# Output projection by seven Strassen products, 512-token blocks with paired PSUM banks, and an interleaved load of batch 1 in a fused attention and bilinear FFN kernel

## The chip, the cores and the metric

The kernel runs on one core of a Trainium2 chip. The metric is the device time of one execution in microseconds (us), given as the median over the runs of one kernel. A run more than 1.5% above the fastest of its kernel is called slow and is left out of every ratio. Two kernels are called different where the interval of the ratio, or the two intervals, leave no room for equality. The engines are PE (TensorE, matmul), PEld (its weight loads, which overlap with PE), DVE (VectorE), ACT (ScalarE), POOL (GpSimd) and SP (SyncE). PE writes its results into PSUM, here eight banks (the tiles `bk`, 128 partitions by 512 float32 values); copying them out to SBUF, where all other tiles lie, is called evacuation. The granted clock is the share of its full clock that the profile shows as granted to PE.

## The reference

The input has 8 batches, 8 heads, 576 positions and a head dimension of 64; the FFN has 4608 tokens, d_model 512 and d_ff 1536.

```python
kv  = einsum('bhsd,bhse->bhde', k, v)
o   = einsum('bhsd,bhde->bhse', q, kv)
x   = o / sqrt(mean(o * o, -1) + 1e-6) * g_norm      # per token and head
x   = x.transpose(0, 2, 1, 3).reshape(4608, 512)
out = ((x @ w_a) * (x @ w_b)) @ w_out                # float32
```

## The kernel before

Attention writes normalised tokens to a ring `xp` (fp16, features on the partitions). The first 512 tokens pass through the FFN in the standard way. The other tokens go in six blocks of 2n tokens, n = 256, 320 or 384, where the two products `x @ w_a` and `x @ w_b` are each computed with seven half-size products instead of eight, in the arrangement by Strassen and Winograd. It needs four sums of weights, made once (`sums`), and four sums of token blocks (`T`), made per block on DVE. The output projection is standard: 12 products of 512 columns per 128 tokens.

Instructions are not issued in the order of the code. Each is a node of a plan with an estimated duration, a priority and its dependencies; a list scheduler (`Plan.order`) fixes the order on each engine at build time. The helper lines under which the profile lists instructions are marked here.

```python
# attention of a late batch: k is reordered on DVE, then K-V, then per head pair and half
r = plan.add("DVE", 1.2, w0, reorder, [(load["n"], 7.0)], [kr], [kb])      # kr_t <- k_t (L556, L559)
n = plan.add("PE", 1.6, w0, kv_mm, [r, (load["n"], 8.0), plan.at(w0 - 3)], [s, kd], [kr, vb])   # L570
#   x_mm (PE L329) -> square (ACT L339) -> mean over head (PE L343) -> rsqrt (ACT L347)
#   -> xp = x * g * rs (DVE L352)
...
first_us = 18.0 if dep is None else 7.0        # batch 2's load has no dep
ld["n"] = plan.add("POOL", first_us, prio, issue, ...)
...
for f0, f1 in zip(WB[:-1], WB[1:]):            # order of the loads: all of w_a, w_b, ...
    nc.gpsimd.dma_start(out=wa_t[:, :, f0:f1], in_=wa_v[:, :, f0:f1])
    nc.gpsimd.dma_start(out=wb_t[:, :, f0:f1], in_=wb_v[:, :, f0:f1])
for i in range(2):                             # ... then batch 1, then w_out
    early_load(early[1], 1, slice(i * HP, (i + 1) * HP))
...
# token sums of a Strassen block, on DVE (L712): T0 = b12-b11, T1 = b22-T0, T2 = b22-b12, T3 = b21-T1
# seven products into banks X, Y, Z of n columns, first for w_a, then for w_b (L734):
p1 = pe(0.0, X, w_lo, fs, lambda: b11, True, xdeps(lo, t0, t0 + n), [X])
e1 = ev(0.0, u1, X, p1)                        # ACT: u1 <- X (L758)
p2 = pe(0.1, Y, w_hi, fs, lambda: b21, True, xdeps(hi, t0, t0 + n), [Y])
c11 = comb(0.1, 0, 0, Y, u1, [p2, e1], ...)    # DVE: abt or b_sb <- Y + u1 (L764)
p6 = pe(0.2, X, sm[1], fs, lambda: tt(1), False, ...)   # goes on accumulating in X
...                                            # p5 in Z, p7 and p4 in X, p3 in Z
nc.vector.tensor_mul(t, t, bb.tile[...])       # abt <- abt * b_sb (L796)
...
# output projection, all blocks (L829), then a copy to SBUF on DVE or ACT (L862) and a store
nc.tensor.matmul(ps.tile[:], lhsT=ab.tile[:, f, g * 128:(g + 1) * 128], rhs=wo_t[:, f, :], ...)
```

Of the kernel before, what the change touches and what calls it, by code (L numbers as in the profile page):

```python
# [40 lines left out]
class Buf:  # L41
# [6 lines left out]
    def take(self, t=0.0):  # L48
        r = self.ring
        i = r.pool.pick()[1]  # L50

        self.tile = r.pool.tiles[i]
        r.pool.holder[i] = self
        r.held = [b for b in r.held if b.freed() > t] + [self]
        return self


class Node:
    def __init__(self, eng, dur, prio, emit, deps=(), takes=(), frees=()):
        self.eng, self.dur, self.prio, self.emit = eng, dur, prio, emit  # L60
        self.deps = [d if isinstance(d, tuple) else (d, None) for d in deps if d is not None]
        self.takes = takes
        self.start = self.end = None
        for b in frees:
            b.last.append(self)


class Plan:
# [29 lines left out]
    def order(self):  # L98
        free, todo, done = {}, sorted(self.nodes, key=lambda n: n.prio), []
        waits = {n: [d for d, _ in n.deps if d.end is None] for n in todo}  # L100
        while todo:
            best = {}
            for n in todo:
                if waits[n]:
                    waits[n] = [d for d in waits[n] if d.end is None]
                    if waits[n]:
                        continue
                f = free.get(n.eng, self.t0)
                if n.eng in best and best[n.eng][0][0] <= f:
                    continue  # L110
                t = max(self.ready(n), f)
                if t == INF:
                    continue
                key = (f if t < f + 0.06 else t, n.prio)
                if n.eng not in best or key < best[n.eng][0]:
                    best[n.eng] = (key, t, n)
            assert best, "no node can go"
            _, t, n = min(best.values(), key=lambda x: x[1])
# [10 lines left out]
def kernel(  # L129
# [27 lines left out]
    WB = [0, 128] + list(range(256, d_ff + 1, 256))  # L157
# [3 lines left out]
    BLOCKS = [(512, 320), (1152, 256), (1664, 320), (2304, 384), (3072, 384), (3840, 384)]  # L161
    NMAX = 384
    NJ = FC // 2

# [5 lines left out]
    def sb(name, shape, dt):  # L170
# [7 lines left out]
    sums = {w: [sb(f"s{w}{i}", [128, 2, HM], FP16) for i in range(4)] for w in "ab"}  # L178
    xp = [sb(f"xp{i}", [128, 2, R], FP16) for i in range(2)]
    k_ts = [sb(f"k_t{i}", [128, H * EC * D], BF16) for i in range(2)]  # L180
    v_ts = [sb(f"v_t{i}", [128, H * EC * D], BF16) for i in range(2)]
# [3 lines left out]
    T_ts = [sb(f"T{i}", [128, 4, 2, NMAX], FP16) for i in range(2)]  # L185
    b_ts = [sb(f"b_sb{i}", [128, 2, 2 * NMAX], FP16) for i in range(2)]
    u_ts = [sb(f"u{i}", [128, NMAX], FP32) for i in range(8)]
    sq_ts = [sb(f"sq{i}", [128, HF], BF16) for i in range(4)]
    rs_ts = [sb(f"rs{i}", [128, HF], FP32) for i in range(4)]
    o_ts = [sb(f"o_sb{i}", [128, d_model], FP32) for i in range(4)]  # L190

    arenas = [
        [ab_ts[1][:].rearrange("p a b -> p (a b)"), 0],
        [T_ts[0][:].rearrange("p a b c -> p (a b c)"), 0],
        [T_ts[1][:].rearrange("p a b c -> p (a b c)"), 0],
        [b_ts[1][:].rearrange("p a b -> p (a b)"), 0],
    ]

    def carve(n, dt=BF16):
        w = n * (2 if dt == FP32 else 1)  # L200
        for a in arenas:
            if a[1] + w <= a[0].shape[1]:
                ap = a[0][:, a[1] : a[1] + w].bitcast(dt)
                a[1] += w
                return ap
        raise ValueError(n)
# [4 lines left out]
    def early_load(t, b, hs):  # L211
        for n, src in (("q", q), ("k", k), ("v", v)):
# [6 lines left out]
        {  # L219
            "q": early_view(carve(H * EC * D)),  # L220
            "k": early_view(k_ts[b]),
            "v": early_view(v_ts[b]),
        }
        for b in range(2)
# [4 lines left out]
    for n, src, eng in (("q", q, nc.scalar), ("k", k, nc.sync), ("v", v, nc.sync)):  # L229
        raw[n] = carve(2 * EC * D, FP32)[0:EP].rearrange("p (h c d) -> p h c d", h=2, d=D)  # L230
# [6 lines left out]
    qs = [[carve(S) for _ in range(NP)] for _ in range(2)]  # L237


    zt = const.tile([128, 512], BF16)  # L240
# [24 lines left out]
    for f0, f1 in zip(WB[:-1], WB[1:]):  # L265
# [3 lines left out]

    for i in range(2):  # L270
        early_load(early[1], 1, slice(i * HP, (i + 1) * HP))
# [128 lines left out]

    N0 = BLOCKS[0][0]

# [58 lines left out]
    def fast_us(n):  # L461
        return (n / 2 + 100) / 960
# [6 lines left out]
    RU, RB, RT, RAB = Ring(u_ts), Ring(b_ts), Ring(T_ts), Ring(ab_ts)  # L469
    RSQ, RRS, ROS = Ring(sq_ts), Ring(rs_ts), Ring(o_ts)  # L470
    RK, RV, RKR, RQT, RKD = Ring(k_ts), Ring(v_ts), Ring([kr_t]), Ring(qT_ts), Ring(kvd[::-1])
# [12 lines left out]
    readers = {}  # L484

# [33 lines left out]
    def early_batch(b, win):  # L519
# [5 lines left out]
        for p in range(NP):  # L525
            pr = w0 + (w1 - w0) * (p - 0.7) / NP
            sq, sk = Buf(RY), Buf(RY)
            here = [plan.at(37.0 if p < NP // 2 else 40.5)]
# [14 lines left out]
    def late_batch(b, load, win):  # L543
# [17 lines left out]
        r = plan.add("DVE", 1.2, w0, reorder, [(load["n"], 7.0)], [kr], [kb])  # L561
        s = Buf(RS)

        def kv_mm():
# [14 lines left out]
            "PE", 1.6, w0, kv_mm, [r, (load["n"], 8.0), plan.at(w0 - 3)], [s, kd], [kr, vb]  # L579
# [14 lines left out]
    def load_node(b, prio, dep):  # L594
# [23 lines left out]
        def transpose():  # L618
# [5 lines left out]
        first_us = 18.0 if dep is None else 7.0  # L624
# [4 lines left out]
            "SP", 2.5, prio, transpose, [(ld["n"], 5.0)], [ld["q"]]  # L629
        )  # L630
        return ld
# [4 lines left out]
    def std_block(win):  # L636
# [4 lines left out]
        rd = readers.setdefault(0, [])  # L641
        for fc in range(2, FC):
            pr = w0 + (w1 - w0) * (fc - 2) / (FC - 2)
            pa, pb = Buf(RX), Buf(RY)

            def mm(ps, w, fc):
# [4 lines left out]
                "PE", mm_us(KC, N0), pr, lambda fc=fc, ps=pa: mm(ps, wa_t, fc), [tk], [pa]  # L651
# [5 lines left out]
                "PE", mm_us(KC, N0), pr + 0.01, lambda fc=fc, ps=pb: mm(ps, wb_t, fc), [tk], [pb]  # L657
# [5 lines left out]
        return ab, muls  # L663

    def weight_sums(prio):
        out = {}
        for w, t in (("a", wa_t), ("b", wb_t)):
            a11, a21 = t[:, 0:2, 0:HM], t[:, 0:2, HM:]
            a12, a22 = t[:, 2:4, 0:HM], t[:, 2:4, HM:]
            s1, s2, s3, s4 = sums[w]  # L670
            for i, (o, x, y, op) in enumerate(
                (
                    (s1, a21, a22, nc.vector.tensor_add),
                    (s2, s1[:], a11, nc.vector.tensor_sub),
                    (s3, a11, a21, nc.vector.tensor_sub),
                    (s4, a12, s2[:], nc.vector.tensor_sub),
                )
            ):
                out[w, i] = plan.add(
                    "DVE", fast_us(2 * HM), prio + 2 * i,  # L680
                    lambda o=o, x=x, y=y, op=op: op(o[:], x, y),  # L681
                    [out[w, i - 1]] if i else [plan.at(32.0)],
                )
        return out

    def wino_block(bi, win, wsum):
        t0, n = BLOCKS[bi - 1]
        w0, w1 = win
        c0 = t0 % R
        b11, b21 = (xp[i][:, :, c0 : c0 + n] for i in range(2))  # L690
        b12, b22 = (xp[i][:, :, c0 + n : c0 + 2 * n] for i in range(2))
        lo, hi = (0, 1), (2, 3)
        rd = readers.setdefault(bi, [])
        tb, ab = Buf(RT), Buf(RAB)
        tk = plan.add("V", 0.0, w0 - 9, lambda: None, (), [ab])

        def tt(i):
            return tb.tile[:, i, :, 0:n]

        t_n = []  # L700
        for i, (x, y, op, pairs, cols) in enumerate(
            (
                (lambda: b12, lambda: b11, nc.vector.tensor_sub, lo, (t0, t0 + 2 * n)),
                (lambda: b22, lambda: tt(0), nc.vector.tensor_sub, hi, (t0 + n, t0 + 2 * n)),
                (lambda: b22, lambda: b12, nc.vector.tensor_sub, lo + hi, (t0 + n, t0 + 2 * n)),
                (lambda: b21, lambda: tt(1), nc.vector.tensor_sub, hi, (t0, t0 + n)),
            )
        ):
            t_n.append(
                plan.add(  # L710
                    "DVE", fast_us(2 * n), w0 - 6 + i,
                    lambda i=i, x=x, y=y, op=op: op(tt(i), x(), y()),  # L712
                    xdeps(pairs, *cols) + ([t_n[0]] if i == 1 else [t_n[1]] if i == 3 else []),
                    [tb] if i == 0 else (),
                )
            )
        rd += t_n
        muls = {}
        for j in range(NJ):
# [5 lines left out]
            outs = []  # L725
            for which, wt in (("a", wa_t), ("b", wb_t)):
                d = 0.01 * "ab".index(which)
                X, Y, Z = Buf(RX), Buf(RY), Buf(RY)
                u1, u2, u3 = Buf(RU), Buf(RU), Buf(RU)
                sm = sums[which]  # L730

                def prod(ps, w, sl, rhs, start):
                    for kc in range(2):
                        nc.tensor.matmul(  # L734
                            ps.tile[:, 0:n],
                            lhsT=w[:, kc, sl],
                            rhs=rhs()[:, kc, :],
                            start=start and kc == 0,
                            stop=kc == 1,
                            skip_group_check=True,  # L740
                        )

                def dst(fi, h, which=which, j=j, bb=bb):
                    hs = slice(h * n, (h + 1) * n)
                    if which == "a":
                        return ab.tile[:, j + fi * NJ, hs]
                    return bb.tile[:, fi, hs]

                def pe(off, ps, w, sl, rhs, start, deps, takes=(), frees=()):
                    return plan.add(  # L750
                        "PE", mm_us(2, n), pr + off + d,
# [182 lines left out]
```

## Time and profile before

| kernel before | |
|---|---|
| time, median (lowest to highest) | 324.19 us (323.47 to 324.8), 4 runs |
| span of the profiled run, mean granted PE clock | 322.0 us, 0.993 |
| PE work by spacing (worked out below) | 294.0 us |
| span less PE work | 28.0 us |

The first line is the busy time of each engine, the other two are the chain of waits that ended last, by engine and by line, all from the profile page of the kernel before.

```profile
PE 307.6 (96%) x2006; PEld 179.2 (56%) x2006; DVE 208.6 (65%) x410; ACT 188.3 (58%) x475; POOL 62.3 (19%) x78
...
PE 86%; DMA 8%; DVE 2%; ACT 2%; issue 1%; DVEq 0%
PE bk L734 45%; PE bk L829 28%; DMA v_t<-in_v_dram 6%; PE bk L393 3%; PE bk L570 3%; PE bk L329 2%; PE bk L343 2%; DMA abt<-in_q_dram 2%; PE bk L287 2%; ACT rs L347 1%; PE bk L317 1%; DVE xp L352 1%; PE bk L301 1%; DVE sa L681 0%; DVE sb L681 0%
```

PE sets the time: it is busy for 96% of the span, and 86% of the chain is PE work. DVE and ACT have a third or more of their time free.

The busy time of PE is not its work, because matmuls overlap. The spacing of back-to-back matmuls is a better measure. This is a line of the timeline of PE at the end of the kernel before (start, length, engine, line, tiles, shape, count):

```profile
314.63 3.62 PE L829 MATMUL bk<-wo_t,abt 128*128 128x512 f16 x16
```

One such matmul takes 381 ns by its group's mean, so the 15 gaps take (3.62 - 0.38) / 15 = 0.216 us each. In the same way 384 columns take 162 ns, 320 take 136, 256 take 109, 288 about 122 and 128 about 61 (the mean over a group of 20 with one change of tile shape in it; 56 between two of the same shape). The "PE work" of a kernel is here the number of its matmuls of each width times these spacings, without the 28 to 30 warm-up matmuls on zeros at the start (L287); the rest of the span is time that PE did not use for it: the start (about 13 us, most of it before the FFN begins at 22 us), the tail and gaps in between.

The largest gap in between is shown by the busy time per engine in stretches of 5 us (stretch, its length, PE, PEld, DVE, ACT and POOL busy with counts, granted clock, DMA share, GB/s):

```profile
50.00:55.00 5.00, 3.54 (x20) 1.76 (x18) 1.68 (x4) 2.15 (x6) 0.00 (x0) 1.00 1.58 192
55.00:60.00 5.00, 2.22 (x20) 1.75 (x20) 1.61 (x4) 0.41 (x1) 0.00 (x0) 0.83 1.40 153
60.00:65.00 5.00, 4.61 (x21) 2.00 (x20) 1.18 (x3) 3.18 (x8) 4.28 (x4) 0.83 0.75 82
```

PE is busy 3.54 and 2.22 us of two stretches, and the granted clock is 0.83 from 55 to 65 us. These are the waits of PE there (what waited, for whom, total us, times, longest):

```profile
PE bk L570 <- DMA v_t<-in_v_dram: 2.1, 1, 2.1
PE bk L329 <- DVE xp L352: 2.1, 1, 2.1
```

### The profile page before, as it was taken

What the parts mean: (1) busy time and instruction counts of PE and PEld (TensorE: products, weight loads), DVE (VectorE), ACT (ScalarE), POOL (GpSimd) and SP (SyncE); (2) the same over time, 40 slices, a digit from 0 to 9 for tenths busy, and PEclk for the clock granted to TensorE, in tenths of its full rate; (3) what the DMA queues carried; (4) which work ended last, traced back from release to release, by engine and by line L of the source; (5) the groups of instructions that cost most, each with busy time, mean ns of one, the idle gap of its engine ahead of it and who ended that gap; (6) DMA issues with size and microseconds to landing.
All of it is one profiled execution on the core that took longest, in us unless ns stands there. A gap on an engine that the chain in (4) does not pass through costs nothing.

```text
span 322.0 us, 5553 instructions
## 1 busy us (share of the span) xinstructions
PE 307.6 (96%) x2006; PEld 179.2 (56%) x2006; DVE 208.6 (65%) x410; ACT 188.3 (58%) x475; POOL 62.3 (19%) x78
## 2 busy tenths in 40 slices
PE   7979996799999999999999999999999999999995
PEld 3434453466666777666666555565555555555542
DVE  3243875179789659866878668687567776646621
ACT  3353373377877666776788556755567656544410
POOL 8855700430802508001600000000000000000000
PEclk9999999799999999999999999999999999999999
DMA  7999999899997999915994100000000200011022
GB/s 159 191 196 199 204 189 182 109 165 180 96 173 94 128 207 127 184 38 108 106 181 74 36 33 33 35 33 35 33 35 35 66 0 35 33 65 36 33 93 103
DMA packets 80235, 32.65 MB, mean 101 GB/s; under 512 B 51920, under 2 KB 75728, under 8 KB 80208
## 3 DMA queue, kind: packets, MB, share of 16 engines
q0 software_dynamic: 59888, 18.44, 52.9%
q1 hardware_dynamic: 19968, 13.44, 17.8%
q10 hardware_dynamic: 352, 0.43, 0.4%
q8 instruction: 15, 0.25, 0.3%
q14 instruction: 12, 0.10, 0.1%
HBM read 37.75 MB, written 12.98 MB: 158 GB/s over the span
## 4 chain that ended last, share of the span: by engine, by line
PE 86%; DMA 8%; DVE 2%; ACT 2%; issue 1%; DVEq 0%
PE bk L734 45%; PE bk L829 28%; DMA v_t<-in_v_dram 6%; PE bk L393 3%; PE bk L570 3%; PE bk L329 2%; PE bk L343 2%; DMA abt<-in_q_dram 2%; PE bk L287 2%; ACT rs L347 1%; PE bk L317 1%; DVE xp L352 1%; PE bk L301 1%; DVE sa L681 0%; DVE sb L681 0%
## 5 line engine op out<-in xcount | busy, mean ns | idle before, releaser
L758 ACT COPY u<-bk 128x384 f32<-128x384 f32 (+2 forms) x216 | 87.8, 448 | 54.6 <-PE bk L734 53.7
L829 PE MATMUL bk<-wo_t,abt 128*128 128x512 f16 x432 | 113.0, 381 | 0.3 <-ACT o_sb L862 0.3
L764 DVE TENSOR_TENSOR abt<-bk,u 128x384 f16<-128x384 f32 (+2 forms) x108 | 55.1, 510 | 49.5 <-ACT u L758 37.5
L829 PEld LDWEIGHTS <-abt 128*128 128x128 f16 x432 | 42.4, 98 | 35.7 <-issue 1.7
L764 DVE TENSOR_TENSOR b_sb<-bk,u 128x384 f16<-128x384 f32 (+2 forms) x108 | 54.6, 505 | 4.7 <-PE bk L734 4.1
L734 PE MATMUL bk<-T,sa 128*128 128x384 f16 (+2 forms) x216 | 48.6, 308 | 0.1
L734 PE MATMUL bk<-T,sb 128*128 128x384 f16 (+2 forms) x216 | 48.2, 308 | 0.0
L352 DVE SCALAR_TENSOR_TENSOR xp<-bk,g_col,rs 128x288 f16<-128x288 f32 x64 | 32.5, 512 | 18.8 <-ACT rs L347 18.8
L734 PEld LDWEIGHTS <-sa 128*128 128x128 f16 x288 | 28.1, 98 | 18.0 <-issue 0.5
L734 PEld LDWEIGHTS <-sb 128*128 128x128 f16 x288 | 28.1, 98 | 17.0 <-issue 0.2
L347 ACT ACTIVATE rs<-bk,eps_t 128x288 f32<-128x288 f32 x64 | 32.3, 508 | 6.8 <-PE bk L343 6.2
L796 DVE TENSOR_TENSOR abt<-abt,b_sb 128x1536 f16<-128x1536 f16 (+2 forms) x36 | 31.3, 870 | 3.7
L734 PE MATMUL bk<-xp,wa_t 128*128 128x384 f16 (+2 forms) x144 | 32.5, 308 | 0.0
L734 PE MATMUL bk<-xp,wb_t 128*128 128x384 f16 (+2 forms) x144 | 32.3, 308 | 0.2 <-ACT b_sb L783 0.2
L339 ACT ACTIVATE sq<-bk 128x288 bf16<-128x288 f32 x64 | 26.1, 419 | 9.2 <-PE bk L329 8.9
L734 PEld LDWEIGHTS <-wa_t 128*128 128x128 f16 x216 | 21.0, 98 | 15.8 <-issue 0.9
L734 PEld LDWEIGHTS <-wb_t 128*128 128x128 f16 x216 | 21.0, 98 | 12.0 <-issue 0.4
L603 POOL DMA_DIRECT2D scr<-in_q_dram x12 | 19.6, 1639 | 3.1 <-issue 2.4
L783 ACT CAST abt<-bk 128x384 f16<-128x384 f32 (+2 forms) x36 | 16.0, 446 | 6.8 <-PE bk L734 6.7
L862 DVE COPY o_sb<-bk 128x512 f32<-128x512 f32 x19 | 13.0, 685 | 9.9 <-PE bk L829 9.7
L862 ACT COPY o_sb<-bk 128x512 f32<-128x512 f32 x16 | 9.4, 588 | 16.5 <-PE bk L829 16.3
L343 PE MATMUL bk<-sq,ones 128*128 128x288 bf16 x64 | 18.5, 289 | 0.6 <-ACT sq L339 0.4
(73 smaller groups left out, 296.1 us busy)
## 6 DMA issues: line engine op xcount, KB each, us to landing
out_dram<-o_sb SPq DMA_DIRECT2D x23, 256.0 KB, 2.0
scr<-in_q_dram POOLq DMA_DIRECT2D x12, 288.0 KB, 6.4
k_t<-in_k_dram POOLq DMA_DIRECT2D x6, 512.0 KB, 9.1
v_t<-in_v_dram POOLq DMA_DIRECT2D x6, 512.0 KB, 11.0
out_dram<-o_sb SPq DMA_DIRECT2D x13, 128.0 KB, 2.3
wo_t<-in_moe_w_out_dram POOLq DMA_DIRECT2D x2, 768.0 KB, 15.4
wa_t<-in_moe_w_a_dram POOLq DMA_DIRECT2D x5, 256.0 KB, 9.1
wb_t<-in_moe_w_b_dram POOLq DMA_DIRECT2D x5, 256.0 KB, 9.7
```

The lines of the kernel that those rows point to most:

```text
L339: nc.scalar.activation(sq, self.x_ps[p, h][:, 0:HF], AF.Square)
L343: nc.tensor.matmul(ps[:, 0:HF], lhsT=ones, rhs=self.sq[p, h], start=True, stop=True)
L347: nc.scalar.activation(rs, self.s_ps[p, h][:, 0:HF], AF.Abs_reciprocal_sqrt, bias=eps_t)
L352: nc.vector.scalar_tensor_tensor(out=xcols(p, self.b * S + h * HF, HF), in0=self.x_ps[p, h][:, 0:HF], scalar=g_col, in1=self.rs[p, h], op0 ...
L603: nc.gpsimd.dma_start(out=scr[:, :, hl, :].rearrange("p s d -> s p d"), in_=qv[hl])
L734: nc.tensor.matmul(ps.tile[:, 0:n], lhsT=w[:, kc, sl], rhs=rhs()[:, kc, :], start=start and kc == 0, stop=kc == 1, skip_group_check=True,)
L758: lambda: nc.scalar.copy(u.tile[:, 0:n], ps.tile[:, 0:n]), [dep], [u],
L764: lambda: nc.vector.tensor_add(dst(fi, h), ps.tile[:, 0:n], u.tile[:, 0:n]),
L783: lambda X=X, dst=dst: nc.scalar.copy(dst(1, 0), X.tile[:, 0:n]),
L796: nc.vector.tensor_mul(t, t, bb.tile[:, :, 0 : 2 * n])
L829: nc.tensor.matmul(ps.tile[:], lhsT=ab.tile[:, order[x], g * 128 : (g + 1) * 128], rhs=wo_t[:, order[x], :], start=x == 0, stop=x == FC - 1,)
L862: eng, us, pr + 0.3, lambda cp=cp, ps=ps, o=os_: cp(o.tile[:], ps.tile[:]),
```

## The change

The intent is to save PE work and to close that gap. Four things change together.

1. The output projection, too, uses seven products (except for the first block): 256 output columns, two token halves. It needs sums of quarters of `w_out` (made once), and four sums of quarters of `abt` per unit of 512 tokens. There are 84 of those of 512 elements on POOL (the last block's twelve are on DVE), because DVE had less room. Of the weight sums, four of 768 elements for `w_a` and four of 1536 elements for `w_out` go to POOL too.
2. All blocks have 512 tokens (n = 256), and a and b share a PSUM bank: one bank holds both halves of 256 columns, so one copy or addition of 512 columns replaces two smaller ones. As before, three banks are attention's and five are for the rest.
3. A copy out of PSUM may go to ACT or DVE; the scheduler picks.
4. The loads of batch 1 stand between those of the weights, and attention of batch 1 may start earlier. Separately, batch 2's load gets a later estimate of its landing (`far`).

The core of the diff (cut; the diff of the helpers for the scheduler, the tile sizes and the early tiles is left out):

```diff
-    WB = [0, 128] + list(range(256, d_ff + 1, 256))
+    WB = [(0, 128), (128, 256)]
+    WB += [(f, f + 256) for f in (768, 256, 1024, 512, 1280)]
+    B1_AT = [24.5, 35.0]
-    BLOCKS = [(512, 320), (1152, 256), (1664, 320), (2304, 384), (3072, 384), (3840, 384)]
+    BLOCKS = [(t, N0 // 2) for t in range(N0, n_tok, N0)]
...
+        if i in (2, 4):
+            early_load(early[1], 1, slice((i // 2 - 1) * HP, i // 2 * HP))
-    for i in range(2):
-        early_load(early[1], 1, slice(i * HP, (i + 1) * HP))
...
+    def either(n, args):
+        return [
+            ("ACT", act_us(n), lambda: nc.scalar.copy(*args())),
+            ("DVE", dve_us(n), lambda: nc.vector.tensor_copy(*args())),
+        ]
...
-        r = plan.add("DVE", 1.2, w0, reorder, [(load["n"], 7.0)], [kr], [kb])
+        r = plan.add("DVE", 1.2, w0, reorder, [(load["n"], 7.0 + load["far"])], [kr], [kb])
-        first_us = 18.0 if dep is None else 7.0
+        first_us, far = (16.0, 10.5) if dep is None else (7.0, 0.0)
...
     def weight_sums(prio, reads):
+                pool = c == 1 and w == "a"          # 4 of the 16 sums, 768 elements each
+                v = nc.gpsimd if pool else nc.vector
...
+    def out_sums(prio):
+        add, sub = nc.gpsimd.tensor_add, nc.gpsimd.tensor_sub
+            ((t3, b22, b12, sub), (b12, b12, b11, sub), (t2, b22, b12, sub), (t4, b21, t2, sub)),
...
     def wino_block(bi, win, wsum):
-                        nc.tensor.matmul(ps.tile[:, 0:n], ...)
+                    for i, (w, sm) in enumerate(wts):       # a and b into one bank
+                        for kc in range(2):
+                            nc.tensor.matmul(ps.tile[:, i * n : (i + 1) * n], ...)
...
+    def o_unit(...):
+        v = nc.vector if eng == "DVE" else nc.gpsimd
+                    (sx(s3), a11, a21, v.tensor_sub, s3),
+                    (a21, a21, a22, v.tensor_add, None),
+                    (sx(s2), a21, a11, v.tensor_sub, s2),
+                    (sx(s4), a12, sx(s2), v.tensor_sub, s4),
...                                                          # p1 ... p7 as in wino_block
-        o_block(bi - 1, ab, muls, (st[bi] + 1.0, st[bi + 1] - 1.0), [RO] * 6)
+            o_block(bi - 1, ab, muls, osum, o_win, "POOL", [(RO, RY, RY)] * 2, 1)
...
+    o_block(nb, ab, muls, osum, (...), "DVE", [(RO, RQ, RQ), (RS, RX, RX)], NJ // 2)
```

## The prediction

> **What bounds the kernel now.** TensorE. The engine table has PE 96% busy; the chain of waits gives PE 86% of the 322.0 us span. From 66 us on PE streams back to back: in the timeline eight 384-column matmuls take 1.30 us (162 ns each), eight of 320 columns 1.09 us (136), eight of 256 columns 0.87 us (109), six of 512 columns 1.29 us (215): columns/2400 us + about 2.5 ns. Weight loads (98 ns each) are hidden, even behind 109 ns. DVE (65%) and ACT (58%) are not the limit.
> With these spacings, PE work after the standard block starts (23.1 us) is: standard block 20.5, FFN Strassen 145.8, output projection 93.0, attention 23.5; together 283 us. The last matmul ends at 318.3, so 12.4 us are lost. The timeline puts nearly all of it at 45-66 us: PE busy 3.5 of 50-55 and 2.2 of 55-60 us (batch 1's normalisation, then batch 2's V, which lands at 58), then a granted clock of 0.83 for 55-65 us.
>
> **What the change does, costed.**
> 1. Output projection: 432 matmuls of 512 columns become 48 of 512 (first block) and 672 of 256: 10.3 + 73.1 = 83.4 us against 93.0: -9.6.
> 2. FFN: same columns, 1344 matmuls of 256 instead of 1008: +0.4.
> 3. Batch 1 lands between the weights, so its attention runs inside the standard block; by the order of instructions about 37 us of PE work (23 to 60 us) now stands ahead of batch 2's K-V product, whose data should land at about 58 as now (same bytes ahead). The loss of 12.4 us should fall to about 3: -9.
> 4. Evacuation: a and b in one bank, so 512-column copies (ACT 0.59 us) and adds (DVE about 0.69) instead of 384 (0.45, 0.51). Per block: DVE about 25 us and ACT 24 us, against 30 us of PE: from about 65% to over 80%, still not the limit, but little slack in five banks.
> 5. New on POOL: 84 sums of 512 elements for the projection, plus weight sums. The Trainium skill, "GPSIMD Engine Reference", section 3 (Performance versus the Vector engine), gives 4497 ns for a 2048-element two-input add: my estimate from it is 1.2 us each, 15 us per block: it fits. No run has shown it. "SBUF — State Buffer", "Who interferes with whom", says a DVE instruction with two SBUF inputs and a GpSimd instruction that reads SBUF block each other. Ten DVE instructions per block have two; estimate: 0.3-0.6 us lost at each hit, partly passed to PE: +3.5 over the run.
> 6. Tail: the last projection is one chain of seven products with one uncovered eviction (about 1 us), and ends in a 512-column add and two 128-row stores: +1.5.
>
> **Sum.** 324.8 - 9.6 + 0.4 - 9 + 3.5 + 1.5 = 311.6; I say 311, range 304 to 319. Faster by over 2%: 0.88; within 2%: 0.10; slower: 0.02.
>
> **What would show it.** Step 1: projection matmuls 109 ns apart. Step 3: no 5 us between 25 and 66 us with PE under 4 us, clock 1.00 there. Step 5: POOL sums of 1.1-1.4 us, DVE products longer than now for their size (1536 elements: 0.96 us) or waiting. Step 6: last matmul 4-5 us before the end.
>
> **What would make it wrong.** POOL sums much slower, or POOL's in-order queue held by the gate on the next batch's loads, so the projection starves PE; DVE or ACT over 90%, so PSUM frees late and PE waits everywhere; weights landing later than the standard block needs.

## The result, and the profile after

| | before | changed |
|---|---|---|
| time, median (range) | 324.19 us (323.47 to 324.8) | 334.84 us (333.74 to 336.24) |
| span of the profiled run, granted clock | 322.0, 0.993 | 332.0, 0.978 |
| PE work by spacing | 294.0 | 285.4 |
| span less PE work | 28.0 | 46.6 |

The changed kernel is slower. The ratio is 1.0332, with a 95% interval of 1.0274 to 1.0389. Ratios in this text are the mean time of one kernel's fast runs over the mean of the other's fast runs of the same rounds, so they are not quite the ratio of the quoted medians.

PE work fell by 8.6 us as planned (the prediction said 9.2), but the unused time rose by 18.6. These are the busy times and the chain of the changed kernel, from its page:

```profile
PE 304.5 (92%) x2628; PEld 241.0 (73%) x2630; DVE 255.1 (77%) x408; ACT 178.7 (54%) x368; POOL 184.8 (56%) x170
...
PE 72%; DVE 20%; issue 3%; ACT 2%; DMA 1%; DVEq 0%; ACTq 0%
PE bk L790 37%; PE bk L951 19%; PE bk L405 6%; DVE c L809 6%; DVE abt L843 3%; DVE xp L364 3%; DVE T L760 2%; PE bk L888 2%; PE bk L341 2%; PE bk L355 2%; DMA so<-in_q_dram 1%; PE bk L299 1%; PE bk L329 1%; DVE xp L760 1%; DVE kr_t L582 1%
```

The chain went from 86% PE to 72%, and DVE went from 2% to 20%. POOL's busy time tripled, from 62.3 to 184.8 us. DVE is busy for 77%, no more than was expected. The longest entries of PE's waits in the changed kernel:

```profile
PE bk L341 <- DVE xp L364: 4.5, 5, 2.7
PE bk L790 <- DVE c L809: 3.8, 10, 0.5
PE bk L790 <- DVE T L760: 3.1, 1, 3.1
PE bk L951 <- DVE abt L843: 3.1, 2, 1.9
```

Every one of these four is a wait for DVE. Now to the groups by shape. First the kernel before, for DVE (line, engine, operation, tiles, shapes, count, busy us, mean ns of one, idle before):

```profile
L796 DVE TENSOR_TENSOR abt<-abt,b_sb 128x1024 f16<-128x1024 f16 x6 | 4.2, 694 | 0.6
...
L712 DVE TENSOR_TENSOR T<-xp,xp 128x512 f16<-128x512 f16 x1 | 0.4, 418 | 0.0
```

The same view of the changed kernel:

```profile
L809 DVE TENSOR_TENSOR c<-bk,u 128x512 f16<-128x512 f32 x144 | 97.0, 684 | 23.6 <-PE bk L790 17.3 <-ACT u L481 5.1 <-ACT c L481 0.3
L843 DVE TENSOR_TENSOR abt<-c 128x1024 f16<-128x1024 f16 x48 | 43.1, 898 | 4.7 <-DVE c L809 0.5
L364 DVE SCALAR_TENSOR_TENSOR xp<-bk,g_col,rs 128x288 f16<-128x288 f32 x64 | 32.1, 510 | 9.8 <-ACT rs L359 9.8
...
L760 DVE TENSOR_TENSOR T<-xp,xp 128x512 f16<-128x512 f16 x16 | 9.2, 576 | 0.4
...
L760 DVE TENSOR_TENSOR T<-xp,T 128x512 f16<-128x512 f16 x8 | 5.0, 631 | 0.2
L760 DVE TENSOR_TENSOR xp<-xp 128x512 f16<-128x512 f16 x8 | 5.0, 631 | 0.2
```

A product of 1024 elements took 694 ns before and takes 898 now; a difference of 512 elements took 418 and takes 576 to 631. The additions out of PSUM (L809) are not in this picture: they take 684 ns, and the attention's `xp` (L364) takes 510, as before (512). Of these, the instructions that grew have both inputs in SBUF; those that didn't have one in PSUM. Not shown: the copies of `k` (L582, one input, in SBUF) grew too, from 339 to 1243 ns. And the means hide that most were untouched: 12 of the 48 products and 8 of the 32 differences took over 0.06 us longer than alone, each of them while a POOL sum ran. A part of the timeline of all engines shows how they grow:

```profile
257.50 1.15 POOL L936 TENSOR_TENSOR as<-abt 128x512 f16<-128x512 f16 x1 [4.00 <-DVE abt L843]
257.88 1.05 DVE L760 TENSOR_TENSOR T<-xp,xp 128x512 f16<-128x512 f16 x1
...
258.73 1.21 POOL L936 TENSOR_TENSOR abt<-abt 128x512 f16<-128x512 f16 x1
258.96 1.25 DVE L760 TENSOR_TENSOR xp<-xp 128x512 f16<-128x512 f16 x1
260.02 1.21 POOL L936 TENSOR_TENSOR as<-abt 128x512 f16<-128x512 f16 x1
260.25 1.25 DVE L760 TENSOR_TENSOR T<-xp,xp 128x512 f16<-128x512 f16 x1
261.31 1.21 POOL L936 TENSOR_TENSOR as<-abt,as 128x512 f16<-128x512 f16 x1
261.54 1.26 DVE L760 TENSOR_TENSOR T<-xp,T 128x512 f16<-128x512 f16 x1
261.56 0.38 PE L790 MATMUL bk<-T,sa 128*128 128x256 f16 x2 [3.15 <-DVE T L760]
```

POOL sums and DVE differences alternate. A difference that takes 0.42 us alone takes 1.25 us, which is the length of a POOL sum, and each starts 0.2 to 0.4 us after a POOL sum does and ends 0.3 us after that sum. PE waits 3.15 us, until the third of the four has ended. The stretch where three long sums of `w_out` run beside two products, 85 to 100 us:

```profile
85.00:90.00 5.00, 3.89 (x46) 3.31 (x43) 5.00 (x7) 3.85 (x10) 4.92 (x3) 1.00 0.19 56
90.00:95.00 5.00, 2.91 (x16) 1.69 (x16) 4.21 (x3) 1.89 (x4) 4.92 (x3) 0.70 0.00 0
95.00:100.00 5.00, 4.37 (x26) 3.27 (x27) 4.86 (x7) 0.90 (x2) 4.84 (x5) 0.62 0.00 0
```

PE is busy 3.89, 2.91 and 4.37 us of three stretches, and the granted clock falls to 0.70 and 0.62. In it the last of the three POOL sums of 1536 elements ran from 91.94 to 95.02 us, and the DVE product that started at 92.02 took 3.56 us.

### The profile page after: what moved, and what is told of

Read it like the earlier page. It is cut to its first block, busy times and chain, and to the rows that moved or that the text cites. A ratio compares the mean times of both kernels' runs of the same rounds, so it can differ in the third digit from the quotient of the medians.

```text
span 332.0 us, 6694 instructions
## 1 busy us (share of the span) xinstructions
PE 304.5 (92%) x2628; PEld 241.0 (73%) x2630; DVE 255.1 (77%) x408; ACT 178.7 (54%) x368; POOL 184.8 (56%) x170
## 4 chain that ended last, share of the span: by engine, by line
PE 72%; DVE 20%; issue 3%; ACT 2%; DMA 1%; DVEq 0%; ACTq 0%
PE bk L790 37%; PE bk L951 19%; PE bk L405 6%; DVE c L809 6%; DVE abt L843 3%; DVE xp L364 3%; DVE T L760 2%; PE bk L888 2%; PE bk L341 2%; PE bk L355 2%; DMA so<-in_q_dram 1%; PE bk L299 1%; PE bk L329 1%; DVE xp L760 1%; DVE kr_t L582 1%
## 5 line engine op out<-in xcount | busy, mean ns | idle before, releaser
L809 DVE TENSOR_TENSOR c<-bk,u 128x512 f16<-128x512 f32 x144 | 97.0, 684 | 23.6 <-PE bk L790 17.3
L936 POOL TENSOR_TENSOR as<-abt 128x512 f16<-128x512 f16 x42 | 51.5, 1226 | 78.4 <-DVE abt L843 61.0
L481 ACT COPY u<-bk 128x512 f32<-128x512 f32 x121 | 69.9, 588 | 46.0 <-PE bk L790 45.2
L790 PE MATMUL bk<-xp,wa_t 128*128 128x256 f16 x288 | 55.4, 274 | 1.7 <-DVE c L809 1.7
L790 PE MATMUL bk<-xp,wb_t 128*128 128x256 f16 x288 | 55.5, 275 | 0.0
L843 DVE TENSOR_TENSOR abt<-c 128x1024 f16<-128x1024 f16 x48 | 43.1, 898 | 4.7 <-DVE c L809 0.5
L951 PE MATMUL bk<-wo_t,abt 128*128 128x256 f16 x288 | 38.4, 280 | 3.1 <-DVE abt L843 3.1
L790 PE MATMUL bk<-T,sa 128*128 128x256 f16 x192 | 37.1, 275 | 3.4 <-DVE T L760 3.1
L364 DVE SCALAR_TENSOR_TENSOR xp<-bk,g_col,rs 128x288 f16<-128x288 f32 x64 | 32.1, 510 | 9.8 <-ACT rs L359 9.8
L790 PE MATMUL bk<-T,sb 128*128 128x256 f16 x192 | 37.1, 276 | 0.0
L951 PEld LDWEIGHTS <-as 128*128 128x128 f16 x288 | 28.4, 99 | 3.6
L936 POOL TENSOR_TENSOR as<-abt,as 128x512 f16<-128x512 f16 x21 | 26.8, 1276 | 7.1 <-PE bk L951 5.8
```

The costliest lines, as they stand in the source:

```text
L364: nc.vector.scalar_tensor_tensor(out=xcols(p, self.b * S + h * HF, HF), in0=self.x_ps[p, h][:, 0:HF], scalar=g_col, in1=self.rs[p, h], op0 ...
L481: ("ACT", act_us(n), lambda: nc.scalar.copy(*args())),
L790: nc.tensor.matmul(ps.tile[:, i * n : (i + 1) * n], lhsT=lhs(w, sm)[:, kc, :], rhs=rhs()[:, kc, :], start=start and i == 0 and kc == 0, st ...
L809: lambda: nc.vector.tensor_add(cs(fi, h), full(ps), u.tile),
L843: nc.vector.tensor_mul(t, c[:, :, :, 0], c[:, :, :, 1])
L936: eng, us, pr - 6 + q, lambda o=o, x=x, y=y, op=op, js=js: op(o(js), x(js), y(js)),
```

## The experiments

Theory A: a POOL instruction that reads SBUF and a DVE instruction with two SBUF inputs exclude each other for their whole duration, and the DVE queue is in order, so each such meeting holds up everything behind it, and PE after that. The Trainium skill, "SBUF — State Buffer", section "Who interferes with whom", states the exclusion and that it does not hold for a POOL instruction that only writes. The rivals: B, DVE simply has too much to do now, or five banks with 512-column evacuations leave PE without a free bank; C, POOL is just late with its sums (they are slow and in order), and PE waits for them; D, the new order of loads does it. Only e4 and e5 keep the order of instructions on PE, DVE and ACT (their traces list the same ones in the same order). In all other runs the scheduler, given other estimates, fixed another order, so what they gain or lose holds the effect of the order too.

### e4_write_only: the same order of instructions, but POOL reads nearly nothing

Each POOL sum becomes a sum of a few columns (237 ns) and two memsets of the whole tile (about 535 ns each for 512 elements), which together take about as long as the sum (1.2 us). The order on PE, DVE and ACT is the same as in the changed kernel.

```diff
+    def wr_only(op):
+        def f(o, x, y):
+            k = (slice(None),) * (len(o.shape) - 1) + (slice(0, 4),)
+            op(o[k], x[k], y[k])
+            nc.gpsimd.memset(o, 0.0)
+            nc.gpsimd.memset(o, 0.0)
+        return f
...
+                if pool:
+                    add, sub = wr_only(add), wr_only(sub)
-        add, sub = nc.gpsimd.tensor_add, nc.gpsimd.tensor_sub
+        add, sub = wr_only(nc.gpsimd.tensor_add), wr_only(nc.gpsimd.tensor_sub)
...                                              # likewise in o_unit
```

> The changed kernel with the order of every engine kept; each POOL sum is replaced by a sum of 4 columns (so that it waits for the same data) and two POOL fills of the same output, which write and do not read. The result is wrong on purpose. Theory A (a POOL instruction that reads SBUF blocks the DVE instructions with two SBUF inputs, and PE waits for the late DVE): the DVE products fall from a mean of 898 to about 690 ns and the differences from 576-631 to about 420 ns, the PE gaps near 53, 93 and 259 us go, and the time falls by 10 to 17 us to 318-325. Rival B (five banks and 512-column evacuation leave too little room, whatever POOL does): DVE still waits for PE and PE for DVE, time within 3 us of 335. Rival C (POOL's sums simply reach PE too late): the fills take about as long, so again within 3 us of 335.

Measured: 317.34 us (315.32 to 317.79), ratio to before 0.9781 (0.9741 to 0.982). That is 0.7 us below the range of theory A. The span is 315.2 us, and POOL is busy for 189.6 us, a little more than in the changed kernel. The DVE groups of this run:

```profile
L820 DVE TENSOR_TENSOR c<-bk,u 128x512 f16<-128x512 f32 x144 | 97.2, 685 | 26.5 <-PE bk L801 19.4 <-ACT u L481 5.4 <-ACT o_sb L994 0.4
L854 DVE TENSOR_TENSOR abt<-c 128x1024 f16<-128x1024 f16 x48 | 33.3, 693 | 4.7 <-ACT u L481 0.5
...
L771 DVE TENSOR_TENSOR T<-xp,xp 128x512 f16<-128x512 f16 x16 | 6.8, 423 | 0.4
...
L771 DVE TENSOR_TENSOR T<-xp,T 128x512 f16<-128x512 f16 x8 | 3.4, 423 | 0.2
```

The products are back at 693 ns and the differences at 423, with POOL just as busy, so it is the reads of POOL that make them long, and not its activity, nor its lateness, nor the order of anything. (The copies of `k` of 64x512 are the exception: 758 ns on the mean here, one of them beside a DMA issue on POOL and the others beside fills, against 278 in e2, where POOL has neither sums nor fills. About 3 us of lengthening stay in e4.) DVE is busy 22.2 us less (232.9 against 255.1) with the same instructions, and the time is 17.5 us shorter: about three quarters of what DVE loses reaches the end. B, C and D cannot give this difference, since the banks, the order on each engine, the loads and POOL's busy time are unchanged. One thing besides the reads is different: the fills are zeros, and PE multiplies them. Whether this raised the granted clock (0.994 against 0.978) was not tried; e2, with right data, has 1.0. The time lost to PE (length of a stretch less the PE work in it; a matmul on an edge is counted on both sides) shows where:

| stretch, us | changed | e4_write_only |
|---|---|---|
| 0 to 40 | 12.7 | 13.1 |
| 40 to 60 | 5.7 | 1.1 |
| 60 to 80 | 0.5 | 0.6 |
| 80 to 100 | 6.7 | 1.0 |
| 100 to 240 | 4.9 | 1.9 |
| 240 to 280 | 6.2 | 1.7 |
| 280 to the end | 7.0 | 6.9 |

Few stretches cost much: those where the weight sums run on POOL (40 to 60, 80 to 100), and one block (240 to 280) in which four sums meet four differences.

### e5_before_pool: POOL sums alone, added to the kernel before

60 sums of 512 elements, which nobody waits for, run on POOL in the kernel before. They read `abt` after each second product. The order of the other engines stays.

```diff
+    junk = [sb(f"junk{i}", [128, 2, 256], FP16) for i in range(4)]
...
+            if j % 2 and bi < len(BLOCKS):
+                for i in range(4):
+                    plan.add("POOL", 1.28, pr + 1 + i, lambda i=i, j=j: nc.gpsimd.tensor_sub(
+                        junk[i][:], ab.tile[:, j-1:j+1, 0:256], ab.tile[:, j-1+NJ:j+1+NJ, 0:256]),
+                        [m], (), [ab])
```

> The kernel before, with the order on PE, DVE and ACT unchanged, plus 60 POOL sums of 512 elements that read the projection's input right after each product and that nothing waits for. Theory A: the products that fall in their time (1536 elements, 0.96 us alone) and the differences take up to 1.2 us more, and the time rises, by less than in the change because DVE has more room here: 1 to 6 us, to 325-331. Rivals B and C: nothing waits for these sums, so no change (within 1 us of 324).

Measured: 332.26 us (331.31 to 333.0), ratio 1.0245 (1.0208 to 1.0282). Sums that nobody waits for cost 8 us, in a kernel where DVE is busy for 65%; theory A had said up to 331. The DVE part of the timeline, where PE then waited 2.72 us:

```profile
91.11 1.25 DVE L713 TENSOR_TENSOR T<-xp,T 128x512 f16<-128x512 f16 x1
92.28 1.37 DVE L713 TENSOR_TENSOR T<-xp,xp 128x512 f16<-128x512 f16 x1
93.57 1.36 DVE L713 TENSOR_TENSOR T<-xp,T 128x512 f16<-128x512 f16 x1
```

The POOL part of the timeline of the same run (three sums shown as one line):

```profile
90.93 3.73 POOL L804 TENSOR_TENSOR junk<-abt 128x512 f16<-128x512 f16 x3 [0.80 <-issue]
```

PE's wait in this run that followed:

```profile
PE bk L735 <- DVE b_sb L765: 2.7, 1, 2.7
```

Three differences took 3.98 us together instead of about 1.25 (three times 0.42). By stretch, about 6.6 us of the added loss lie in 80 to 100 us (0.8 before, 3.7 here) and 120 to 140 us (0.4 and 4.2), where three differences in a row met POOL sums; from 160 us on, where sums run as well, nothing was lost. So it is not the sum that costs but a sum that meets a chain of differences just before PE needs them. The products of 1536 elements did not grow here (959 ns in both kernels): POOL's sums wait for a product, so they start after it. Theory A had expected them to.

### e1_sums_dve, e3_as_dve and e2_all_dve: which of the sums

e1 puts only the eight long weight sums on DVE; e3 puts only the 84 sums per block on DVE; e2 puts all there.

```diff
e1:  -                pool = c == 1 and w == "a"
     +                pool = False
     -        add, sub = nc.gpsimd.tensor_add, nc.gpsimd.tensor_sub      # out_sums; "POOL" -> "DVE"
     +        add, sub = nc.vector.tensor_add, nc.vector.tensor_sub
e3:  -            o_block(bi - 1, ab, muls, osum, o_win, "POOL", [(RO, RY, RY)] * 2, 1)
     +            o_block(bi - 1, ab, muls, osum, o_win, "DVE", [(RO, RY, RY)] * 2, 1)
e2:  both
```

> The changed kernel, with only the weight sums (FFN and projection) moved from POOL to DVE; the 84 sums per block stay on POOL. Theory A: the long sums (3.1-3.4 us each) caused the gaps at 53 and 92 us and the two clock drops after them, so 6 to 10 us of the loss go: 325-329. If the sums per block do most of the harm: within 3 us of 335.

> The changed kernel with only the 84 per-block sums moved to DVE; the eight long weight sums (1.6-3.4 us each) stay on POOL. Moving only the long ones gained 1.4 us of the 12.9 us that moving all gained. If the per-block sums hold nearly all the harm: 322-325. If either set alone is enough to keep DVE late at the block boundaries (the harms overlap): above 328.

> The changed kernel with every POOL sum moved to DVE (0.42 us each there): POOL only issues DMA. DVE gains about 35 + 8 us of work and loses about 26 us of blocked time. Theory A: no DVE instruction is lengthened, time 314-321, below the kernel before. Rival B (DVE and the banks are the limit): more DVE work makes it slower still, above 335. Rival C: also faster, about as theory A says.

Measured: e1 333.42 us (ratio 1.0289), e3 336.5 us (1.0371), e2 321.92 us (0.9934, interval 0.9911 to 0.9957). Theory A's value for e1 was missed: moving the long sums alone gains little (by the ratios 0.4%, within the intervals). The time fell in the other branch, but its reading, that the sums per block do most of the harm, is not borne out by e3. e3 gains nothing at all over the changed kernel (the intervals overlap: 1.0323 to 1.0419 against 1.0274 to 1.0389). Yet both together gain 13 us, so what the two kinds of sums cost does not add up. e3 shows one reason. The timeline of DVE in e3:

```profile
85.87 3.19 DVE L936 TENSOR_TENSOR as<-abt 128x512 f16<-128x512 f16 x1
89.10 3.19 DVE L936 TENSOR_TENSOR as<-abt,as 128x512 f16<-128x512 f16 x1
92.21 3.30 DVE L936 TENSOR_TENSOR as<-abt 128x512 f16<-128x512 f16 x1
```

The timeline of POOL in e3 at the same time:

```profile
85.67 3.11 POOL L695 TENSOR_TENSOR wo_t<-wo_t 128x1536 f16<-128x1536 f16 x1 [13.71 <-PE bk L888]
88.87 3.14 POOL L695 TENSOR_TENSOR so<-wo_t 128x1536 f16<-128x1536 f16 x1
92.08 3.14 POOL L695 TENSOR_TENSOR so<-wo_t,so 128x1536 f16<-128x1536 f16 x1
```

Three DVE sums that take 0.42 us each alone took 9.68 us, one for each long POOL sum, and PE had one wait of 7.7 us for the attention's `xp` behind them. With the 84 sums per block gone from POOL, three of the eight that remain cost that much, because DVE now has many sums of its own with two SBUF inputs that can meet them. e2 has no POOL reads, and no DVE group is long (products 692 ns, differences 420 to 424). It was 0.9 us above the upper end of what theory A expected, and 4.6 us slower than e4; DVE now does 84 more sums of 0.42 us itself. DVE is as busy in e2 as in the changed kernel (256.5 us against 255.1), and e2 is 13 us faster, so how much DVE does is not what made the changed kernel slow (rival B).

### e7_e2_old_loads and e10_before_far: what closed the gap at 45 to 66 us

e7 is e2 with batch 1 loaded after all the weights, as before. e10 is the kernel before with only the later estimate of batch 2's landing.

```diff
e7:  +    WB += [(f, f + 256) for f in (256, 512, 768, 1024, 1280)]
     +    B1_AT = [37.0, 40.5]
     +    for i in range(2):                                   # after the weights
     +        early_load(early[1], 1, slice(i * HP, (i + 1) * HP))
     (cut: the planned times of the weights and the order of the first block follow)
e10: -        r = plan.add("DVE", 1.2, w0, reorder, [(load["n"], 7.0)], [kr], [kb])
     +        r = plan.add("DVE", 1.2, w0, reorder, [(load["n"], 7.0 + load["far"])], [kr], [kb])
     -        first_us = 18.0 if dep is None else 7.0
     +        first_us, far = (16.0, 10.5) if dep is None else (7.0, 0.0)
     (and far in the deps of kv_mm and of the transposing load)
```

> The version with all sums on DVE (321.9 us), with batch 1 loaded after all the weights again, as before the change. If loading it between the weights is worth what I read from the trace (the loss between 40 and 70 us is about 7 us smaller without POOL's sums): 327-330, and PE gaps near 50-60 us come back. If the gap there had another cause: 321-323.

> The kernel before, with one thing of the change: the planned landing of batch 2's first load moved later (10.5 us more), so that DVE's reordering of batch 2's K stands after batch 1's normalisation in DVE's queue instead of ahead of it. In the trace of before that reordering holds DVE's queue until K lands at 54.3 us, and PE waits. If the loss at 45-66 us came from this queue position, not from when the data land: the gap there shrinks from about 8 us to 1-3 us and the time falls to 317-320. If it came from the order of the loads (my prediction): no change, 323-325.

Measured: e7 322.8 us (ratio 0.9947, 0.9917 to 0.9977), against e2's 0.9934: the order of the loads is worth 0.4 us by the ratios, which the intervals don't separate from nothing. e10 318.18 us (0.9804, 0.9782 to 0.9827), 6.4 us faster than before. The stretches of e10, to be set against those of before:

```profile
50.00:55.00 5.00, 4.56 (x25) 2.30 (x24) 2.95 (x7) 3.35 (x10) 0.00 (x0) 1.00 1.57 193
55.00:60.00 5.00, 4.87 (x26) 2.43 (x25) 3.01 (x8) 2.35 (x7) 0.00 (x0) 1.00 1.14 213
```

PE is busy 4.56 and 4.87 us where it was busy 3.54 and 2.22, and the clock stays at 1.00. Two in-order queues were held in the kernel before. First, DVE's, in its timeline:

```profile
54.27 0.69 DVE L556 COPY kr_t<-k_t 128x2048 bf16<-128x2048 bf16 x1 [3.29 <-DMA k_t<-in_k_dram]
...
55.09 0.93 DVE L352 SCALAR_TENSOR_TENSOR xp<-bk,g_col,rs 128x288 f16<-128x288 f32 x2
```

The reorder of batch 2's `k` stood ahead of batch 1's last normalisations in DVE's in-order queue, because the plan thought that its data would have landed. DVE sat for 3.29 us waiting for the load while work behind it was ready, and PE waited 2.1 us for that work. In e10 that work comes first and the reorder starts at 58.11 us without a wait. `k` landed no earlier (54.4 us against 54.3).

Second, PE's own. The edit also moves batch 2's K-V product. Before, it stood next in PE's queue and waited 2.1 us for `v`, with matmuls of the projection behind it; in e10 those go first and it starts 3 us later, without a wait. PE's timeline before, then in e10:

```profile
58.06 2.25 PE L570 MATMUL bk<-v_t,kr_t 128*128 128x128 bf16 x20 [2.14 <-DMA v_t<-in_v_dram]
...
61.04 1.38 PE L570 MATMUL bk<-v_t,kr_t 128*128 128x128 bf16 x20
```

So the position in both queues closed the gap. How much belongs to each was not tried.

### e8_std_dve, e9_all_dve_tuned, e11_e2_act and e13_std_tuned: what the projection by seven products is worth

e8 takes the standard projection back with all else of the change, and no POOL sums. e9 is e2 with five choices of the plan changed. e11 is e2 with only the first of them. e13 is e8 with those of them that exist there.

```diff
e9:  -            ("DVE", dve_us(n), lambda: nc.vector.tensor_copy(*args())),   # copies on ACT only
     -                    eng, us, pr - 6 + q, ...                 # sums of abt 8 us later in the order
     +                    eng, us, pr - 6 + q + (8), ...
     -    late_us = 3.0                                            # less extra time planned per block
     +    late_us = 1.0
     -        at_win[b] = (max(61.0, st[...] + ... - 10), ...)     # attention starts earlier
     +        at_win[b] = (max(61.0, st[...] + ... - 14), ...)
     -    O_A, O_B = 12.0, 3.0                                     # projection 3 us later
     +    O_A, O_B = 15, 3
e11: only the first of these
e8:  o_block(...) -> o_std(bi - 1, ab, muls, o_win, [RO] * 4), with 12 products of 512 columns
     per 128 tokens; no out_sums; O_A, O_B = 1.0, -1.0; weight sums on DVE
e13: e8 with the first, the third and the fourth of e9's
```

> Strassen's products for the projection undone (432 matmuls of 512 columns again, no sums of activations or of the projection's weights), everything else as in the version with all sums on DVE: 512-token blocks, shared banks, batch 1 early. PE has 9 us more work, DVE about 45 us less. If five banks and 512-column evacuation are themselves a limit (rival B), PE still has gaps all along and the time is 325 or more. If they are not, PE streams and the time is 316-320, below both kernels.

> All sums on DVE as in e2, but the 21 copies that DVE took from ACT go back to ACT (58% busy), the sums per block stand 8 us later in the order, and four other offsets of the order are changed. DVE falls from 80% to about 76% of the span. If what is left of the loss in e2 is DVE coming late at block boundaries, the time falls to 312-318, below the kernel before; if it is the five banks: 320-323.

> All sums on DVE (e2, 321.9 us), with the 21 copies that DVE took from ACT given back to ACT, and nothing else. If DVE's load was what held e2 back, most of the 9.5 us between e2 and the tuned version appear: 313-317. If the place of the sums in the order was: 319-322.

> The standard output projection (all eight block products, no weight sums and no token sums for it) with everything else of the change, no sums on GpSimd, and the tuned copies and orders of e9 as far as they exist here. It needs about 9 us more of PE spacing than e9 (294.9 against 285.4 us). If Strassen's projection is worth its PE work once VectorE is relieved: 318 to 322 us, that is 6 to 9 us behind e9. If VectorE's sums for it eat the gain also in the tuned order: 312 to 315 us, within 1% of e9.

| | time, us | ratio to before | PE work | span less PE work | DVE busy |
|---|---|---|---|---|---|
| e2 (seven products) | 321.92 | 0.9934 | 285.4 | 34.5 | 80% |
| e8 (standard) | 322.71 | 0.9942 | 294.9 | 26.8 | 69% |
| e9 (seven products, tuned) | 312.46 | 0.9631 | 285.4 | 25.3 | 80% |
| e13 (standard, tuned) | 320.82 | 0.991 | 294.9 | 23.7 | 61% |

In the order of the change, the seven products gained nothing without POOL (e2 against e8): in the profiled spans, 7.7 of the 9.5 us of PE work came back as waiting. The expectation for e8 was missed, as its value lay between the branches. With the copies and the order tuned, they are worth 8.4 us (312.46 against 320.82; by the ratios 2.9%), and e13 fell where the first branch had it. But the tuning was made for e9, and e13 is not the best kernel with the standard projection: e10, with the old blocks, takes 318.18 us, 5.7 us more than e9 (by the ratios 1.8%). That e8 and e13 are slower than e10 (ratios 0.9942 and 0.991 against 0.9804), with 0.9 us more of PE work, suggests that the new blocks and banks have a price; as loads and order differ too, this was not separated. e9 beats the kernel before by 3.7% (interval of its ratio 0.9589 to 0.9672), and so the changed kernel too. The busy line of e9:

```profile
PE 296.2 (95%) x2630; PEld 238.5 (77%) x2630; DVE 247.9 (80%) x470; ACT 192.2 (62%) x398; POOL 62.4 (20%) x78
```

The time of e9 lies in the first branch of its expectation; DVE, though, is busy for 80% of the span and not for about 76%. DVE's own work is larger than in the changed kernel (247.9 us, against the 232.9 that e4 shows for the same instructions with little lengthening), and PE gets its 285.4 us of work into 310.7. So the amount of work on DVE was not the limit as such. (The expectation counts four other offsets; the edit changes three.) e11 gave 318.05, 319.66 and 318.05 us in fast runs (ratio 0.9819, 0.9785 to 0.9853) and one slow run of 448.43 us, in which the profile fell, so its trace is not used. It lies between the two branches. Between e2 and e9 the copies give 3.7 us by the ratios and the other choices the rest, 6.1; which of those matters was not tried.

### e12_pool_tuned: the tuned order with the sums on POOL

```diff
(the five edits of e9, with "POOL" kept for the sums in weight_sums, out_sums and o_block)
```

> The changed kernel with all POOL sums kept on POOL, but with the same choices as the tuned version (copies on ACT, sums 8 us later, the other four offsets). DVE has 20 to 40 us less to do than in the tuned version. If DVE's load or the order was the real trouble of the change: 310-314, as fast as the tuned one or faster. If the blocking of DVE by POOL's reads is: DVE products and differences stay lengthened, 322-332.

Measured: 320.98, 320.94 and 322.47 us in fast runs (ratio 0.9907, 0.9875 to 0.994); the profiled run was slow (326.09), so only durations of single instructions are read from it: products 860 ns, differences 594 to 635 ns. The products of e12, to be set against 692 ns alone:

```profile
L842 DVE TENSOR_TENSOR abt<-c 128x1024 f16<-128x1024 f16 x48 | 41.3, 860 | 5.7 <-ACT u L481 1.0
```

In the text of the kernels e9 and e12 differ only in the engine of the sums (the scheduler then fixes another order), and e12 is 9 us slower (means of the fast runs 321.5 and 312.5), just below the range of the second branch. So with the tuned choices, too, the sums cost more on POOL than on DVE, although DVE does them itself in e9. The same choices gain 13 us over the changed kernel with all sums still on POOL (ratio 0.9907 against 1.0332): what the meetings cost depends on where they fall, and 17.5 us is the cost in the order of the changed kernel.

## Why the prediction was wrong

The prediction was 311 us with a range of 304 to 319 and 88% for faster; the changed kernel took 334.84. Point by point:

- **"What bounds the kernel now": right.** PE did; the gap at 45 to 66 us was found, but its cause was not (below).
- **Step 1, the output projection, -9.6, and step 2, FFN, +0.4: right for PE's work.** 285.4 against 294.0 is -8.6, and 256-column matmuls run 109 ns apart. What it saves reached the end only with the copies and the order tuned (e2 against e8, e9 against e13).
- **Step 3, batch 1 between the weights, -9: the gain was there, its size and cause were off.** "The loss of 12.4 us should fall to about 3" was credited to the order of loads. e10 got 6.4 us with one estimate of the plan and the old loads, and e7 lost 0.4 us, within the intervals, by going back to them. The position in two in-order queues was the cause: DVE's stood for 3.29 us at a copy whose data had not landed, and PE's for 2.14 us at the product behind it, which waited for `v`. The prediction did say that more PE work would stand ahead of that product, but took it for an effect of the loads; and for DVE's queue it had followed PE's wait for the normalisation back only one step. In the changed kernel 40 to 60 us still lose 5.7 us, because weight sums on POOL moved in there; without their reads (e4) it is 1.1.
- **Step 4, evacuation in five banks, "still not the limit, but little slack", no term: a small term was missing.** e4 has no POOL reads, and its span less PE work is 29.8 us, 1.8 above before. With the gap's -5.5 (e10's profiled span, 316.5, against 322.0; by the medians -6.4) and the tail's +2.9 in it, about 4.4 are left over for many small waits in five banks; this is by subtraction, not shown one by one. e8 and e13, which have the new blocks and banks but the standard projection and are slower than e10, point the same way. e9, which has 25.3, shows that other copies and another order avoid most of it.
- **Step 5, the POOL sums, "0.3-0.6 us lost at each hit, partly passed to PE: +3.5 over the run": the step that failed.** The sums took 1.18 to 1.28 us as estimated, and the meeting was foreseen and its kind was right. Its price was mis-sized: +17.5 us (changed against e4), five times the term. There were three errors in it. The price of a hit was about right for most, but not for all: beside sums of 512 elements the products that were hit lost 0.5 us on average and the differences 0.7 (0.83 where the whole difference was held up, 0.42 to 1.25), but two products beside sums of 1536 elements lost 1.9 and 2.9 us. "Ten DVE instructions per block" left out the copies of `k` (nine were lengthened) and DVE's own weight sums (three): these are 10.3 us of DVE's lost time, against 15.7 for the products and differences. (By stretch, 40 to 60 and 80 to 100 us, where the weight sums run, hold 10.3 of the 17.5.) And "partly passed to PE" took DVE's free time, a fifth of the span, for slack at every place; but the differences come in a chain right before PE needs them, and three quarters of DVE's 22.2 us reached the end, not the small part that +3.5 stands for. Where PE waited long, the granted clock dropped as well: 0.70 and 0.62 from 90 to 100 us.
- **Step 6, the tail, +1.5: too small.** The timeline of PE at the end shows waits of 1.20 us for a DVE product and 0.67 us for an ACT copy in the last projection, and the last matmul ends 4.7 us before the end instead of 3.7: +2.9.

The ledger from profiled spans: 322.0 - 8.6 (PE work) - 5.5 (gap, if it closes as in e10) + 2.9 (tail) + 4.4 (small waits, by subtraction) = 315.2, the span of e4; with the reads of POOL +16.8 it is 332.0, the span of the changed kernel. The chance of 2% for "slower" was far too low: "POOL sums much slower" stood among the things to go wrong, but not that they would hold up DVE.

## What to carry to other kernels

Don't move a two-input sum to POOL because DVE looks full, before you know what on DVE has two SBUF inputs: each meeting can make a DVE instruction as long as the POOL one, and what counts is whether PE waits for the chain in which it stands. Here the same sums cost 9 us less on a DVE that was busy for 80% than on POOL. And look at what an in-order queue is waiting for when work behind it is ready: moving one copy and one product a few places gave 6.4 us, and the best kernel with seven products is only 5.7 us faster than that (e9 against e10).

## What the Trainium skill lacked or had wrong

- "SBUF — State Buffer", section "Who interferes with whom", is right in what these runs test (POOL reads lengthen DVE's products and differences, e4's writes don't, additions with one input in PSUM stay at 684 ns; five copies of `k` are longer beside e4's writes too, 424 to 694 ns against 278). It lacks what this looks like and costs: in the profile the blocked instruction is not shown as waiting but as long, 0.42 us becomes 1.25 or 3.2 us, and chains on both engines alternate in lockstep, so that a chain of four differences takes as long as four POOL sums.
- "Perfetto Trace Analysis", section "Optimizing Scalar/DVE Operations", says that moving work between DVE and POOL "might not help". Here it harmed: the tuned kernel takes 312.5 us with the sums on DVE and 321.5 with the sums on POOL, and 60 sums that nobody waits for cost 8 us in the kernel before.
- "GPSIMD Engine Reference", section 3 (Performance versus the Vector engine): its 4497 ns for 2048 elements gave a good estimate (1.2 us for 512 elements measured, 3.1 to 3.4 us for 1536). The comparison there counts only POOL's own time, not what DVE loses in it: 22.2 us of DVE's time here.
- "TensorE: Matmul & The Clock Gate", section "Back-to-back issue gap", gives sustained spacings of about 131 ns for 512 columns and 81 ns for 128 with weight loads between. These runs show 216 ns and 56 ns (61 as the mean over a group), with a weight load for each matmul of the projection. That is near its formula for an isolated gap (N/2.4 + 2.5 ns: 215.8 and 55.8), and not near the sustained figures.
